# Strided and local attention ahead of an expert layer: products with v in 64x64 tiles, two pieces to a burst, with scores in bursts of their own

## The chip, the cores and the metric

One core of one Trainium2 chip runs the whole program. The metric is the device time of one execution in microseconds, the median of three runs. The matrix engine (TensorE) is PE in the rows.

## What is computed

Eight batches of 576 tokens with eight heads of 64 are attended to, four heads with a local mask (a query sees itself and the 31 keys before it) and four with a strided mask (a query sees keys at or before it in the same residue modulo 32). The result, 4608 rows of 512, goes through a two-matrix layer with a smooth gate.

```python
    mask_local = (rel >= 0) & (rel < stride)
    mask_strided = (rel >= 0) & (pos[None, :] % stride == pos[:, None] % stride)
    ...
    scores = np.where(masks[None, :, :, :], scores, -1000000000.0)
    scores = scores - np.max(scores, axis=-1, keepdims=True)
    attn = np.exp(scores)
    attn = attn / (np.sum(attn, axis=-1, keepdims=True) + 1e-09)
    return np.matmul(attn, v).astype(np.float32)
...
    h = x @ w_in
    sp = np.maximum(h, 0.0) + np.log1p(np.exp(-np.abs(h)))
    g = h * erf(sp)
    return (g @ w_out).astype(np.float32)
```

## The kernel before

**The layer.** The rows are taken in 12 chunks of 384, and the hidden width of 2048 in 16 steps of 128. A chunk and a step make an `ftile`: `mm1` (12 matmuls of 384 columns: high and low parts of x and of the weight), a chain of eight steps that ScalarE (ACT) and VectorE (DVE) do in turn, and three `mm2` jobs of three matmuls of 512 columns, which add up in one bank per 128 rows. 192 ftiles run in all. The x of a chunk lies in `xhi` and `xlo`, a ring of two batches.

**The weights** come as pairs of 32-bit words. For each of 32 weight tiles (`weight`) DVE does `bits0`, `bits1` and `bits2`, ACT the high part, and DVE the low part (`split_lo_w`, which writes `pair`).

**The attention** is cut into six pieces to a batch: local pieces of two blocks of 96 queries against 128 keys, and strided pieces of two blocks of seven residues (126 queries and keys) and a last one of four residues. A piece holds four heads, two on the partitions (`h`) and two side by side (`i`). The twelve pieces of the first two batches (`head`) run while the weights are loaded. The other 36 (`quad`) run among the ftiles of earlier batches. A quad goes: scores on PE (line 327, or line 312 for the last strided piece), `mask` (DVE), `maxi` (GpSimd, POOL), `sub` (DVE), `exp` (ACT), `total` (POOL), `gather`, `invert` and `spread` (DVE), the products with v on PE (`av`, line 574, tile `x`), `scale` (DVE), and per pair of heads a high part (ACT) and a low part (DVE) into the ring.

**The order.** `Plan.order` walks all operations with planned durations and due times (`HK`, `GK`, `WK`, ...) and writes one order for each engine; an engine never departs from it at run time. Where PE has nothing planned ahead of the first `mm1`, the plan puts in `warm` matmuls. In a quad the products of the piece before and the scores of the next are one job, so that they stand side by side:

```python
            def burst():
                yield from before.av()
                yield from g.scores()
```

**The banks.** Two banks (`ps`) take scores, three (`h`) take the results of `mm1` and the products `x`, and three take the sums of `mm2`. Scores run as 64x64 tiles of the array (64 rows of q and k for one head, 64 keys), products as 128x64 tiles (128 keys, 64 values of one head).

Of the kernel before, what the change touches and what calls it, by code (L numbers as in the profile page):

```python
# [19 lines left out]
P = 128  # L20
CH = 384
# [11 lines left out]
WK = (68.9352, -179.94, -4.88482, -99.4542, 101.236, 96.6232, -88.8363, 94.4097, 145.483, 133.702, 121.816, 123.575, 147.426, 102.135, 159.432, 198.004, -50.7856, -9.1942, 6.38548, 86.1292, 102.234, 0.760304, 78.3002, 56.9697, 173.822, 137.573, 106.312, 217.753, 188.75, 198.944, 228.222, 217.783)  # L33
LD = (5.82581, -62.2561, -111.18)
HD = (-24.4811, -111.662, -129.595, -53.3828, -157.869, -21.6826, -158.891, -9.78484, -7.41211, -95.013, -64.0153, -4.18983)
HK = (10.9721, -123.087, -70.0383, -13.5816, 91.4778, 39.4063, 92.0314, 93.8213, 94.7931, 115.323, 121.42, 178.387)
GK = (32.6682, 31.3304, 33.8245, 38.4663, 38.8279, 43.8312, 47.6315, 49.4667, 53.9059, 59.3896, 61.1923, 65.5209, 63.8285, 72.2803, 72.1316, 75.437, 80.7086, 86.9161, 80.8736, 95.711, 101.92, 105.262, 109.74, 109.871, 115.411, 120.755, 121.654, 126.517, 130.466, 137.372, 136.019, 146.264, 153.723, 151.754, 162.279, 163.399)
QD = (-3.67373, 14.2205, -4.5465, 1.44199, -4.58934)
ADT = -0.840127
PF = -5.56049  # L40
BACKLOG = 3.44486
FT = (-1.5755, -14.4223, 3.35947, -5.55073, -22.2539, 3.41975, -8.81461, 1.84242, -9.78646)
# [7 lines left out]
WE = 2 * (S - 4 * QS) + P  # L50
WV = 2 * 2 * (D + 1)
# [65 lines left out]
class Plan:  # L117
# [9 lines left out]
    WINDOW = 70  # L127
# [77 lines left out]
def attention_moe(  # L205
# [23 lines left out]
    xhi = [cpool.tile([P, RING], F32R, name=f"xhi{c}") for c in range(NCC)]  # L229
    xlo = [cpool.tile([P, RING], F32R, name=f"xlo{c}") for c in range(NCC)]  # L230
# [4 lines left out]
    cap = cpool.tile([P, 368], BF16, name="cap")[:, : 2 * QL + QS]  # L235
    cap_l = cap[:, : 2 * QL].rearrange("p (b h q) -> p b h q", b=2, h=1)
    cap_s = cap[:, 2 * QL :].rearrange("p (u q) -> p u q", u=1)
# [32 lines left out]
    def group(b, loc, j, bank="ps", spare=None):  # L270
# [20 lines left out]
        s = [buf("ps_" + bank, bank, [P, 512], f"s{i}_{pid}") for i in range(nbank)]  # L291

# [69 lines left out]
        def views(px, i, t):  # L362
            base, src = (b % 2) * S, px[:, i * w : (i + 1) * w]
            if loc:
                c0 = base + j * 2 * QL
                return src, t[:, c0 : c0 + w]
            r0 = 2 * RB * j
            dst = t[:, base : base + S].rearrange("p (a r) -> p a r", r=32)[:, :, r0 : r0 + w // NA]
            return src.rearrange("p (r a) -> p a r", a=NA), dst

        def split(px, i):
            def split_hi():
                src, hi = views(px, i, xhi[hps[i]])
                yield nc.scalar.copy(hi, src)

            def split_lo_x():
                src, hi = views(px, i, xhi[hps[i]].bitcast(F32))
                _, lo = views(px, i, xlo[hps[i]])
                yield nc.vector.tensor_tensor(out=lo, in0=src, in1=hi, op=ALU.subtract)

            return split_hi, split_lo_x
# [9 lines left out]
    def head(b, loc, j, key, dt, early, bank, num, sub_pe_too, norm_act):  # L391
# [13 lines left out]
        pt = buf("ps_h", "h", [P, 512], f"t_{pid}")  # L405
# [97 lines left out]
        done = []  # L503
        for i in range(2):
            hi, lo = g.split(pt, i)
            o = add("act", act(w, 0.07), key + 2 * dt + 0.1, hi, [o_t], [], [pt])
            done.append(add("dve", dve(w), key + 2 * dt + 0.2, lo, [o], [], [pt]))
        return done

    def quad(b, loc, j, key, dt, before):  # L510

        g = group(b, loc, j)
        n, nblk, nbank, cols, w, s, sm, pid = g.n, g.nblk, g.nbank, g.cols, g.w, g.s, g.sm, g.pid
        mx = [buf("apool", "mx", [P, 512], f"mx{i}_{pid}") for i in range(nbank)]
        su = [buf("apool", "mx", [P, 512], f"su{i}_{pid}") for i in range(nbank)]
        pos = 32 * (-(-n // 32))
        width = 32 * (-(-cols // 32)) if nbank == 2 else 2 * pos
        tt = buf("apool", "tt", [P, 512], f"tt_{pid}")
        inv = buf("apool", "tt", [P, 512], f"inv_{pid}")
        rc = buf("zpool", "r", [P, 16, 1], f"r_{pid}")  # L520
        px = buf("ps_h", "h", [P, 512], f"x_{pid}")

        def mask(k):
            def run():
                r, z, m = g.masks(k, cap_l, cap_s)
                yield nc.vector.tensor_tensor(  # L526
                    out=sm[k][:, :cols].rearrange(r, **z), in0=s[k][:, :cols].rearrange(r, **z), in1=m, op=ALU.min
                )

            return named("mask", run)  # L530

# [6 lines left out]
        def gather(h):  # L538

            def run():  # L540
                rows, t = slice(h * D, (h + 1) * D), su[h % nbank]
                tail = width - cols if nbank == 2 else pos - n
                if tail:
                    yield nc.vector.memset(t[rows, cols : cols + tail], 1.0)
                if nbank == 2:
                    yield nc.vector.transpose(tt[rows, :width], t[rows, :width])  # L546
                    return
                for u in range(2):
                    lo = (2 * u + h) * n
                    yield nc.vector.transpose(tt[rows, u * pos : (u + 1) * pos], t[rows, lo : lo + pos])  # L550

            return named("gather", run)
# [9 lines left out]
        def spread():  # L562
            nb = width // 32
            yield nc.vector.transpose(
                inv[:, :width].rearrange("p (c k) -> p c k", k=32), rc[:, :nb].broadcast_to([P, nb, 32])
            )

        def av():
            for i in range(2):
                for blk in range(nblk):  # L570
                    for h in range(2):
                        bank, c = g.place(i, blk, h)
                        c0 = (i * nblk + blk) * n
                        yield nc.tensor.matmul(  # L574
                            px[h * D : (h + 1) * D, c0 : c0 + n], g.vpart(i, blk, h, D), sm[bank][:, c : c + n],
                            start=True, stop=True,
                        )

        def scale():
            yield nc.vector.tensor_tensor(  # L580
                out=px[:, : 2 * w].rearrange("p (u q) -> p u q", q=n),
                in0=px[:, : 2 * w].rearrange("p (u q) -> p u q", q=n),
                in1=inv[:, : 2 * w].rearrange("p (u q) -> p u q", q=n) if nbank == 2
                else inv[:, :width].rearrange("p (u q) -> p u q", q=pos)[:, :, :n],
                op=ALU.mult,
            )

        add = plan.add
        lq, lv = loads(g, key)
        d_s = (0.76 if loc else 0.79) if nblk == 2 else 0.625  # L590
        d_v = (1.005 if n > QL else 0.8) if nblk == 2 else 0.39
        if before:
            def burst():
                yield from before.av()
                yield from g.scores()

            o_s = add("pe", d_s + before.d_v, key, burst, [lq, *before.need], [before.px, *s, *sm], [g.qk, *before.use])
            before.finish(o_s)
        else:
            o_s = add("pe", d_s, key, g.scores, [lq, *o_con], [*s, *sm], [g.qk])  # L600
        o_e = []
        for k in range(nbank):
            o = add("dve", dve(cols), key + 0.1 + 0.01 * k, mask(k), [o_s], [], [s[k], sm[k]])
            o = add("pool", 0.4 + cols * 0.0028, key + 0.2 + 0.01 * k, g.maxi(k, mx[k]), [o], [mx[k]], [sm[k]], earliest=6.7)
            o = add("dve", dve(cols), key + QD[0] * dt + 0.01 * k, g.sub(k, mx[k]), [o], [], [mx[k], sm[k]])
            o_e.append(add("act", act(cols), key + QD[0] * dt + 0.1 + 0.01 * k, g.exp(k), [o], [], [sm[k]]))
        o_g = []
        for k in range(nbank):
            o = add("pool", 0.094 + cols * 0.0063, key + QD[1] * dt + 0.01 * k, total(k), [o_e[k]], [su[k]], [sm[k]])
            o_g.append(o)  # L610
        n_g = (1 if nbank == 2 else 2) * 0.06 + width / 960.0 + (0.16 if cols % 32 else 0.1)
        o = None
        for h in range(2):
            k = h % nbank
            o = add("dve", n_g, key + QD[2] * dt + 0.01 * h, gather(h), [o_g[k]] + ([o] if o else []), [tt, inv] if h == 0 else [], [su[k], tt])
        o = add("dve", 0.36, key + QD[2] * dt + 0.05, invert, [o], [rc], [tt])
        o_i = add("dve", dve(width), key + QD[2] * dt + 0.06, spread, [o], [], [rc, inv])
        done = [[], []]

        def finish(o_v):  # L620
# [217 lines left out]
    def load_consts():  # L838
        yield nc.scalar.dma_start(con_f[:, :NCON], consts)
# [215 lines left out]
```

## Time and profile before

| what | value |
|---|---|
| median of three runs | 920.48 us (920.34 to 920.9) |
| span of the profiled execution | 919.3 us |
| matmuls busy (PE) | 910.6 us, 99% |
| DVE, ACT, POOL busy | 675.9, 573.0, 313.7 us |
| products with v (line 574), matmul records | 528 |
| `warm` matmuls ahead of the first `mm1` | 134 |

The span runs from the first to the last recorded instruction. What lies around it in a timed run is the difference to the median, 1.2 us. A line number is that of the kernel of the rows.

### The profile page before, as it was taken

How to read it: one execution, taken by the hardware profiler on the slowest of the kernel's cores; microseconds unless marked ns; L12 is line 12 of the kernel's file. 1: busy time of each engine (PE TensorE's matmuls, PEld its weight loads, DVE VectorE, ACT ScalarE, POOL GpSimd, SP SyncE). 2: the span in 40 equal slices, each digit the busy share in tenths (PEclk: the TensorE clock that was granted, in tenths of full speed). 3: DMA queues.
4: the chain of work that ended last, by engine and by line, in shares of the span. 5: the costliest groups of instructions: out<-in, count | busy, mean ns of one | idle time of the engine just before them, and what ended most of it. 6: DMA issues, size and time to landing. Idle time of an engine off the chain costs nothing.

```text
span 919.3 us, 16608 instructions
## 1 busy us (share of the span) xinstructions
PE 910.6 (99%) x6273; PEld 813.4 (88%) x6273; DVE 675.9 (74%) x1473; ACT 573.0 (62%) x1279; POOL 313.7 (34%) x158
## 2 busy tenths in 40 slices
PE   8999999999999999999999999999999999999998
PEld 5888999988888898889889889898989989899997
DVE  5999999678878777687767767777766767755553
ACT  4777676656566656566566556656656655655654
POOL 4341101243735346347214425373431443300000
PEclk9999999999999999999999999999999999999999
DMA  9974011221112013112102011120210210000001
GB/s 351 391 264 143 12 58 35 92 89 47 61 41 78 17 45 99 32 37 88 52 0 71 25 62 54 47 65 32 59 42 1 75 61 13 35 1 1 35 0 35
DMA packets 25712, 63.15 MB, mean 69 GB/s; under 512 B 2848, under 2 KB 4256, under 8 KB 25632
## 3 DMA queue, kind: packets, MB, share of 16 engines
q1 hardware_dynamic: 25488, 61.86, 19.8%
q8 instruction: 49, 0.80, 0.3%
q14 instruction: 31, 0.25, 0.1%
q10 hardware_dynamic: 144, 0.23, 0.1%
HBM read 51.07 MB, written 11.01 MB: 68 GB/s over the span
## 4 chain that ended last, share of the span: by engine, by line
PE 95%; DVE 3%; ACT 1%; DMA 0%; issue 0%; POOL 0%; DVEq 0%
PE o L764 42%; PE h L701 42%; PE x L574 3%; PE ps L327 2%; PE warm L936 2%; PE av L435 1%; DVE a L706 1%; PE ps L423 0%; PE ps L312 0%; PE s L423 0%; DMA qk<-qk_loc 0%; DVE sm L351 0%; PE ps L411 0%; PE t L470 0%; PE ps L435 0%; DVE w L660 0%
## 5 line engine op out<-in xcount | busy, mean ns | idle before, releaser
L709 ACT ACTIVATE a<-a 128x384 f32<-128x384 f32 x576 | 294.7, 523 | 114.5 <-DVE a L706 105.6
L764 PE MATMUL o<-pair,ghi 128*128 128x512 f32 x1154 | 359.6, 393 | 0.0
L706 DVE SCALAR_TENSOR_TENSOR a<-a,h 128x384 f32<-128x384 f32 x384 | 209.9, 549 | 140.4 <-ACT a L709 138.0
L701 PE MATMUL h<-xhi,pair 128*128 128x384 f32 x1536 | 300.1, 338 | 0.3 <-DVE glo L736 0.3
L701 PEld LDWEIGHTS h<-xhi,pair 128*128 128x128 f32 x1536 | 269.8, 188 | 10.0 <-DVE glo L736 1.7
L344 POOL PARTITION_ALL_REDUCE mx<-sm x88 | 135.3, 1560 | 414.1 <-DVE sm L526 334.2
L764 PEld LDWEIGHTS o<-pair,ghi 128*128 128x128 f32 x1154 | 212.9, 188 | 38.3
L764 PE MATMUL o<-pair,glo 128*128 128x512 f32 x577 | 224.7, 389 | 0.0
L534 POOL PARTITION_ALL_REDUCE su<-sm x66 | 178.5, 2740 | 73.5 <-ACT sm L358 48.7
L709 ACT ACTIVATE a<-h 128x384 f32<-128x384 f32 x192 | 94.2, 491 | 132.3 <-PE h L701 128.4
L701 PE MATMUL h<-xlo,pair 128*128 128x384 f32 x768 | 164.5, 336 | 0.0
L730 DVE TENSOR_TENSOR h<-a,h 128x384 f32<-128x384 f32 x192 | 106.9, 557 | 44.2 <-ACT a L709 43.6
L701 PEld LDWEIGHTS h<-xlo,pair 128*128 128x128 f32 x768 | 136.0, 188 | 0.0
L764 PEld LDWEIGHTS o<-pair,glo 128*128 128x128 f32 x577 | 108.4, 188 | 23.1
L736 DVE TENSOR_TENSOR glo<-h,ghi 128x384 fp32r<-128x384 f32 x192 | 105.9, 552 | 24.6 <-ACT ghi L733 21.2
L733 ACT CAST ghi<-h 128x384 fp32r<-128x384 f32 x192 | 90.8, 473 | 45.3 <-PE o L764 28.4
L358 ACT ACTIVATE sm<-sm 128x384 f32<-128x384 f32 (+2 forms) x77 | 42.0, 553 | 13.5 <-DVE sm L351 13.2
L351 DVE TENSOR_TENSOR sm<-sm,mx 128x384 f32<-128x384 f32 (+2 forms) x77 | 46.7, 614 | 0.1
L546 DVE STREAM_TRANSPOSE tt<-su 64x384 f32<-64x384 f32 (+1 forms) x60 | 37.4, 624 | 5.3 <-POOL su L534 2.2
L526 DVE TENSOR_TENSOR sm<-ps,cap 128x384 f32<-128x384 f32 (+2 forms) x66 | 37.4, 587 | 3.6 <-PE ps L327 2.3
L574 PEld LDWEIGHTS x<-sm,v 128*64 128x64 f32 x528 | 24.6, 136 | 9.8 <-issue 8.4
L574 PE MATMUL x<-sm,v 128*64 128x96 f32 (+2 forms) x528 | 31.7, 260 | 0.0
(62 smaller groups left out, 451.8 us busy)
## 6 DMA issues: line engine op xcount, KB each, us to landing
v<-v_all SPq DMA_DIRECT2D x40, 260.0 KB, 3.8
qk<-qk_loc SPq DMA_DIRECT2D x24, 416.0 KB, 3.4
out<-ob SPq DMA_DIRECT2D x35, 256.0 KB, 2.0
words<-w_in SPq DMA_DIRECT2D x16, 512.0 KB, 7.1
words<-w_out SPq DMA_DIRECT2D x16, 512.0 KB, 7.3
qk<-qk_str SPq DMA_DIRECT2D x16, 508.0 KB, 3.8
qk<-qk_str SPq DMA_DIRECT2D x8, 272.0 KB, 3.1
part<-ob SPq DMA_DIRECT2D x6, 256.0 KB, 2.0
```

Source lines behind the costliest of these rows:

```text
L344: yield nc.gpsimd.partition_all_reduce(mx[:, :cols], sm[k][:, :cols], P, ReduceOp.max)
L351: yield nc.vector.tensor_tensor(out=d, in0=d, in1=mx[:, :cols], op=ALU.subtract)
L358: yield nc.scalar.activation(d, src[:, :cols] if src else d, AF.Exp, scale=1.0 / D**0.5)
L534: yield nc.gpsimd.partition_all_reduce(su[k][:, :cols], sm[k][:, :cols], P, ReduceOp.add)
L574: yield nc.tensor.matmul(px[h * D : (h + 1) * D, c0 : c0 + n], g.vpart(i, blk, h, D), sm[bank][:, c : c + n], start=True, stop=True,)
L701: yield nc.tensor.matmul(ph[:, :CH], win[4 * s + cc][:, w, fs], x[cc][:, c0 : c0 + CH], start=(i == 0), stop=(i == len(terms) - 1))
L706: yield nc.vector.scalar_tensor_tensor(out=out, in0=in0, scalar=scalar, in1=in1, op0=op0, op1=op1)
L709: yield nc.scalar.activation(dst, src, func, bias=bias[i], scale=scale)
L730: yield nc.vector.tensor_tensor(out=ph[:, :CH], in0=a.tile, in1=ph[:, :CH], op=ALU.mult)
L733: yield nc.scalar.copy(ghi.tile, ph[:, :CH])
L736: yield nc.vector.tensor_tensor(out=glo.tile, in0=ph[:, :CH], in1=ghi.tile.bitcast(F32), op=ALU.subtract)
L764: yield nc.tensor.matmul(po[:, half], g[:, ts], wout[f][:, w, half], start=(f == fs0 and i == 0), stop=(f == fs1 and i == 2 and half.stop ...
```

## The change

Only quads change in what they compute with; a head merges two writes into one.

- Strided pieces have two blocks of six residues (108 queries) for the first two and two blocks of four (72 queries) for the third, so that all six pieces have two blocks and two banks. The keys of a block lie in two halves of 64 partitions, three (or two) residues in each, padded with zeros.
- Scores are 16 matmuls a piece in 64x64 tiles of 64 columns (local), 54 or 36 (strided). They are written with the key half outermost, where it was inside the block. They are a PE job of their own.
- The products of two pieces are one PE job (`products`): 16 matmuls a piece with 64 keys against 64 values, of 64, 54 or 36 columns. Each key half goes to a bank of its own, and these are the two `ps` banks. For a local piece the middle 32 queries of a block get a share from both halves: ACT copies one (`mid`), DVE adds it (`join_mid`).
- `scale` and the splits run per key half. The factors overwrite `tt`, and `inv` is gone. The ring tiles hold two pairs of heads each, so one split serves both.
- The caps come with a DMA of their own (`load_caps`). All due times are new, as is the planner's look-ahead.

```diff
+QB = 6 * NA
+HB = QB // 2
...
+        meet = ((0, 64), (32, 96)) if loc else ((0, nh), (nh, n))
...
+        def scores():
+            for part in range(2):
+                for u in range(4):
+                    i, blk = u // 2, u % 2
+                    cq, ck = i * wq + blk * n, i * wq + 2 * n + blk * (n if loc else P) + part * 64
+                    for h in range(2):
+                        rows = slice(h * D, (h + 1) * D)
+                        q0, q1 = meet[part]
+                        yield nc.tensor.matmul(
+                            s[h][part * 64 : (part + 1) * 64, u * n + q0 : u * n + q1],
+                            qk[rows, ck : ck + 64], qk[rows, cq + q0 : cq + q1],
+                            start=u == 0, stop=True, skip_group_check=True,
+                        )
...
-        if before:
-            def burst():
-                yield from before.av()
-                yield from g.scores()
-
-            o_s = add("pe", d_s + before.d_v, key, burst, [lq, *before.need], [before.px, *s, *sm], [g.qk, *before.use])
...
+        o_s = add("pe", 0.75, key, scores, [lq, *o_con, *last], [*s, *sm], [qk])
...
+    def products(pair, key, dt):
+
+        px = [buf("ps_ps", "ps", [P, 512], f"x{p}_{pair[0].b}_{pair[0].loc}_{pair[0].j}") for p in range(2)]
+
+        def av():
+            for m, g in enumerate(pair):
+                for u in range(4):
+                    for h in range(2):
+                        for p, (q0, q1) in enumerate(((0, g.na), (g.n - g.na, g.n))):
+                            rows = slice(p * 64, (p + 1) * 64)
+                            yield nc.tensor.matmul(
+                                px[p][h * D : (h + 1) * D, m * 256 + u * g.na : m * 256 + (u + 1) * g.na],
+                                g.v[rows, (2 * u + h) * (D + 1) : (2 * u + h) * (D + 1) + D],
+                                g.sm[h][rows, u * g.n + q0 : u * g.n + q1],
+                                start=True, stop=True,
+                            )
...
+        def mid(m, g):
+            def run():
+                yield nc.scalar.copy(
+                    g.tt[:, 384:512].rearrange("p (u q) -> p u q", u=4),
+                    px[1][:, m * 256 : (m + 1) * 256].rearrange("p (u q) -> p u q", u=4)[:, :, :32],
+                )
...
+        def join_mid(m, g):
+            def run():
+                x = cells(px, m, g, 0)[:, :, 32:]
+                yield nc.vector.tensor_tensor(out=x, in0=x, in1=g.tt[:, 384:512].rearrange("p (u q) -> p u q", u=4), op=ALU.add)
...
+            for p in range(2):
+                cols = 4 * (g.nb if p else g.na)
+                o = add("dve", dve(cols), key + QD[3] * dt + 0.12 + 0.01 * m, scale(m, g, p), first if p == 0 else first[:2], [], [px[p], g.tt])
+                hi, lo = split(m, g, p)
+                o = add("act", act(cols, 0.07), key + QD[4] * dt + 0.13 + 0.01 * m, hi, [o], [], [px[p]])
+                g.done[1].append(add("dve", dve(cols), key + QD[4] * dt + 0.2 + 0.01 * m, lo, [o], [], [px[p]]))
...
-WK = (68.9352, -179.94, -4.88482, -99.4542, 101.236, 96.6232, -88.8363, 94.4097, 145.483, 133.702, 121.816, 123.575, 147.426, 102.135, 159.432, 198.004, -50.7856, -9.1942, 6.38548, 86.1292, 102.234, 0.760304, 78.3002, 56.9697, 173.822, 137.573, 106.312, 217.753, 188.75, 198.944, 228.222, 217.783)
+WK = (67.5487, -148.418, 36.8869, -154.672, -255.399, 110.018, 123.581, 130.519, 16.7657, 222.711, 198.383, 120.355, 197.321, 285.192, 240.069, 207.216, -156.292, 104.167, 46.9332, -6.25954, 76.5432, 148.16, 110.823, 161.074, -20.4493, 274.699, 209.259, 238.497, 314.036, 347.411, 319.306, 420.096)
```

Where the order puts things, at the three places that matter. First PE at the start, in the kernel before: the last stretch ahead of the first `mm1` (`t` is a head's transposed result, `qk_2_0` belongs to the second batch, `warm` is a filler).

```order
L411 MATMUL ps_94<-con 128x504
...
L936 MATMUL warm<-con 128x256
...
L470 MATMUL t_2_2_771<-ident,xn_0_2_2_709 128x72
L470 MATMUL t_2_2_771<-ident,xn_0_2_2_715 128x72
...
L701 MATMUL h_804<-xhi_81,pair_744 128x384
```

The same place in the changed kernel (line 437 is a head's product with v, here of the third local piece of the first batch, and line 472 its transpose).

```order
L437 MATMUL av_0_0_2_654<-v_0_2_239,sm_0_2_468 96x65 x4
...
L413 MATMUL ps_90<-con 128x384
L791 MATMUL h_697<-xhi_81,pair_628 128x384
...
L472 MATMUL t_0_2_725<-ident,xn_0_0_2_646 128x96 x2
L472 MATMUL t_0_2_725<-ident,xn_0_0_2_655 128x96 x2
L332 MATMUL ps_89<-qk_2_0_507 64x72
```

The transposes of that piece and the scores of the second batch's first strided piece (with their mask matmuls) moved from ahead of the first `mm1` to behind it. Over the whole stretch 104 `warm` stand where 134 stood. On DVE, 66 instructions stand ahead of the low part of the first weight tile of block 0 (`pair0`, which that `mm1` reads) where 83 stood: 8 weight tiles are finished there instead of 10, four `invert` instructions fewer and half as many splits.

Second, PE among the ftiles. In the kernel before, a quad's products and the next quad's scores (`x_0_1` is the product of a local piece):

```order
L701 MATMUL h_2357<-xlo_88,pair_1887 128x384
L574 MATMUL x_0_0_2375<-sm_2_0_0_1559,v_0_0_2082 64x96
L574 MATMUL x_0_0_2375<-sm_2_0_0_1560,v_0_0_2082 64x96
...
L327 MATMUL ps_94<-qk_0_1_1155 64x64
L327 MATMUL ps_93<-qk_0_1_1155 64x64
```

In the changed kernel the scores of the two strided pieces of a pair have six rows (nine matmuls) of `mm2` between them:

```order
L542 MATMUL ps_89<-qk_False_2599 64x54
L854 MATMUL o_2_0_2595<-pair_1100,ghi_2857 128x512 x2
L854 MATMUL o_2_0_2595<-pair_1100,glo_2866 128x512
L854 MATMUL o_2_0_2603<-pair_1100,ghi_2857 128x512 x2
L854 MATMUL o_2_0_2603<-pair_1100,glo_2866 128x512
L854 MATMUL o_2_0_2617<-pair_1100,ghi_2857 128x512 x2
L854 MATMUL o_2_0_2617<-pair_1100,glo_2866 128x512
L542 MATMUL ps_90<-qk_False_2674 64x36
```

Both scores write the same two banks (`ps_89`, `ps_90`). Products and scores no longer stand side by side anywhere: 36 bursts of scores and 18 of products are each set between matmuls of the layer. Counted in an ftile's `mm1` or its three `mm2` as one step, the products stand 4 to 16 steps behind the pair's second scores, and the next scores 3 to 19 steps behind the products. Ten of the 18 pairs have only one such step between their two scores.

Third, DVE between a pair's products and the next scores, in the changed kernel (`ps_90` and `ps_89` hold the products; lines 820, 826 and 796 belong to ftiles, line 557 is the mask of the next scores).

```order
L675 TENSOR_TENSOR ps_89<-ps_89,tt_False_7754 128x216
L820 TENSOR_TENSOR h_7822<-a_7856,h_7822 128x384
L796 SCALAR_TENSOR_TENSOR a_7895<-a_7895,h_7843 128x384
L607 STREAM_TRANSPOSE tt_False_7801<-r_False_7904 128x288
L701 TENSOR_TENSOR xlo_84<-ps_90,xhi_82 128x2x18x6
L675 TENSOR_TENSOR ps_90<-ps_90,tt_False_7801 128x144
L675 TENSOR_TENSOR ps_89<-ps_89,tt_False_7801 128x144
L701 TENSOR_TENSOR xlo_84<-ps_89,xhi_82 128x2x18x6
...
L701 TENSOR_TENSOR xlo_84<-ps_89,xhi_82 128x2x18x4
...
L557 TENSOR_TENSOR sm_7_True_7966<-ps_90,cap 128x384
```

Before, the products lay in an `h` bank, and a scale and two splits (lines 580 and 379) stood here for one piece, with the mask of the next scores ahead of the splits. Now all scales and splits of two pieces stand ahead of the next scores' mask, since the banks are the same.

## Rows read from the trace of the kernel before

**Rows 1.** The page: busy time, share of the span and instructions of each engine.

```profile
PE 910.6 (99%) x6273; PEld 813.4 (88%) x6273; DVE 675.9 (74%) x1473; ACT 573.0 (62%) x1279; POOL 313.7 (34%) x158
```

**Rows 2.** The page: the chain that ended last, by engine.

```profile
PE 95%; DVE 3%; ACT 1%; DMA 0%; issue 0%; POOL 0%; DVEq 0%
```

**Rows 3.** Windows: stretch, length, busy us of five engines, granted clock, DMA share.

```profile
40.00:48.00 8.00, 8.00 (x128) 6.92 (x128) 7.86 (x25) 7.16 (x24) 1.65 (x2) 1.00 1.01 383
185.00:400.00 215.00, 215.00 (x1576) 191.50 (x1575) 163.57 (x363) 130.92 (x290) 105.70 (x51) 1.00 0.18 57
```

**Rows 4.** Timeline of PE around 450 us: start, length, line, operation, shape, count.

```profile
443.92 0.39 PE L764 MATMUL o<-pair,glo 128*128 128x512 f32 x1
444.24 1.08 PE L574 MATMUL x<-sm,v 128*64 128x126 f32 x16
445.26 0.76 PE L312 MATMUL ps<-qk 128*128 128x144 f32 x4
445.76 1.66 PE L701 MATMUL h<-xhi,pair 128*128 128x384 f32 x8
...
452.12 0.47 PE L574 MATMUL x<-sm,v 128*64 128x72 f32 x8
452.52 0.69 PE L327 MATMUL ps<-qk 64*64 64x64 f32 x32
453.15 1.66 PE L701 MATMUL h<-xhi,pair 128*128 128x384 f32 x8
```

**Rows 5.** Timeline of PE at the last products burst.

```profile
799.11 0.88 PE L574 MATMUL x<-sm,v 128*64 128x96 f32 x16
799.92 0.72 PE L764 MATMUL o<-pair,ghi 128*128 128x512 f32 x2
800.49 0.40 PE L764 MATMUL o<-pair,glo 128*128 128x512 f32 x1
800.72 0.62 PE L764 MATMUL o<-pair,ghi 128*128 128x512 f32 x2
801.18 0.39 PE L764 MATMUL o<-pair,glo 128*128 128x512 f32 x1
```

**Rows 6.** PE from 185 to 805 us by form: count, busy us, mean ns.

```profile
L574 PE MATMUL x<-sm,v 128*64 128x96 f32 x288 | 15.9, 252 | 0.0
L574 PE MATMUL x<-sm,v 128*64 128x126 f32 x192 | 13.0, 277 | 0.0
```

**Rows 7.** Timeline of PE up to the first mm1.

```profile
43.10 0.50 PE L470 MATMUL t<-ident,xn 96*128 96x96 f32 x4
43.43 0.68 PE L435 MATMUL av<-v,sm 128*72 128x65 f32 x8
44.03 0.72 PE L327 MATMUL ps<-qk 64*64 64x72 f32 x32
...
45.12 1.15 PE L936 MATMUL warm<-con 128*128 128x256 bf16 x9
46.10 0.29 PE L470 MATMUL t<-ident,xn 72*128 72x72 f32 x2
...
47.68 1.65 PE L701 MATMUL h<-xhi,pair 128*128 128x384 f32 x8
```

**Rows 8.** Timeline of DVE at the same place.

```profile
47.81 0.67 DVE L674 TENSOR_TENSOR pair<-w,pair 128x512 fp32r<-128x512 f32 x1
```

**Rows 9.** DVE from 14 to 185 us by form: count, busy us, mean ns.

```profile
L674 DVE TENSOR_TENSOR pair<-w,pair 128x512 fp32r<-128x512 f32 x32 | 23.2, 724 | 1.4 <-ACT pair L671 1.4
...
L653 DVE TENSOR_SCALAR w<-words 128x512 uint32<-128x512 uint32 x30 | 13.5, 460 | 0.1
```

**Rows 10.** Line 574: when its semaphore waits were taken up.

```profile
L574 PE MATMUL x<-sm,v x528: 226/246/323, 188.2 to 799.7; 128*64 128x96 f32 x96, 128*64 128x126 f32 x64, 128*64 128x72 f32 x16
L574 PEldq EVENT_SEMAPHORE  x36: 51/51/665, 185.3 to 795.9; - x36
```

**Rows 11.** Timeline of DVE behind the scores burst of 452.52.

```profile
453.27 1.02 DVE L526 TENSOR_TENSOR sm<-ps,cap 128x384 f32<-128x384 f32 x2
```

More of the change, by code (lines that the diff above doesn't have):

```diff
@@ L126 @@
     ENTER = 0.08
-    WINDOW = 70
+    WINDOW = 400
     def __init__(self, bufs):
@@ L502, in head @@
         o_t = add("pe", 0.22 * nblk, key + 2 * dt, transp, o_n, [pt], xn_b)
[L503 to L517, printed above, removed]
+        o = add("act", act(2 * w, 0.07), key + 2 * dt + 0.1, g.split_hi, [o_t], [], [pt])
@@ new lines, in head, with quad @@
+        return [add("dve", dve(2 * w), key + 2 * dt + 0.2, g.split_lo_x, [o], [], [pt])]
+    def quad(b, loc, j, key, dt, load, last):
+        n = QL if loc else (QB if j < 2 else 4 * NA)
+        w, cols, nh = 2 * n, 4 * n, n // 2
+        pid = f"{b}_{loc}_{j}"
+        wq = WL if loc else 2 * n + 2 * P
+        wv = 4 * (D + 1)
+        width = 32 * (-(-cols // 32))
+        na, nb = (64, 32) if loc else (nh, nh)
+        qk = buf("apool", "qk", [P, 2 * WS], f"qk_{pid}")
+        v = buf("zpool", "v", [P, 2 * WV], f"v_{pid}")
+        s = [buf("ps_ps", "ps", [P, 512], f"s{i}_{pid}") for i in range(2)]
+        sm = [buf("apool", "sm", [P, 512], f"sm{i}_{pid}") for i in range(2)]
+        mx = [buf("apool", "mx", [P, 512], f"mx{i}_{pid}") for i in range(2)]
+        su = [buf("apool", "mx", [P, 512], f"su{i}_{pid}") for i in range(2)]
@@ L523, in mask @@
         def mask(k):
             def run():
[L525 to L528, printed above, removed]
-            return named("mask", run)
+                d, x = sm[k][:, :cols], s[k][:, :cols]
+                if loc:
+                    m = (cap_l if j == 0 else cap_l[:, 1:2]).rearrange("p b h q -> p h b q").broadcast_to([P, 2, 2, n])
+                    d, x = (y.rearrange("p (i b q) -> p i b q", i=2, b=2) for y in (d, x))
+                else:
+                    m = cap_s.rearrange("p (u t q) -> p u t q", u=1, t=2)[:, :, :, :nh].broadcast_to([P, 4, 2, nh])
+                    d, x = (y.rearrange("p (u t q) -> p u t q", u=4, t=2) for y in (d, x))
@@ L532, in total, with exp, run @@
+        def exp(k):
+            def run():
+                d = sm[k][:, :cols]
+                yield nc.scalar.activation(d, d, AF.Exp, scale=1.0 / D**0.5)
+            return named("exp", run)
         def total(k):
@@ L540, in run @@
             def run():
[L541 to L550, printed above, removed]
+                rows, t = slice(h * D, (h + 1) * D), su[h]
+                if width > cols:
+                    yield nc.vector.memset(t[rows, cols:width], 1.0)
+                yield nc.vector.transpose(tt[rows, :width], t[rows, :width])
             return named("gather", run)
@@ L564, in spread @@
             yield nc.vector.transpose(
[L565 to L585, printed above, removed]
+                tt[:, :width].rearrange("p (c k) -> p c k", k=32), rc[:, :nb].broadcast_to([P, nb, 32])
@@ L601, in quad @@
-        o_e = []
[L602 to L606, printed above, removed]
+        lq = add("sp", P * 8 * wq / 3.6e5, load - LD[0], load_qk, new=[qk])
@@ new lines, in quad @@
+        lv = add("sp", P * 8 * wv / 3.6e5, load - LD[1], load_v, new=[v])
+        o_s = add("pe", 0.75, key, scores, [lq, *o_con, *last], [*s, *sm], [qk])
+        o_e = []
+        for k in range(2):
+            o = add("dve", dve(cols), key + 0.1 + 0.01 * k, mask(k), [o_s, *o_cap], [], [s[k], sm[k]])
+            o = add("pool", 0.4 + cols * 0.0028, key + 0.2 + 0.01 * k, maxi(k), [o], [mx[k]], [sm[k]])
+            o = add("dve", dve(cols), key + QD[0] * dt + 0.01 * k, sub(k), [o], [], [mx[k], sm[k]])
+            o_e.append(add("act", act(cols), key + QD[0] * dt + 0.1 + 0.01 * k, exp(k), [o], [], [sm[k]]))
@@ L607, in quad @@
         o_g = []
[L608 to L611, printed above, removed]
+        for k in range(2):
+            o_g.append(add("pool", 0.094 + cols * 0.0063, key + QD[1] * dt + 0.01 * k, total(k), [o_e[k]], [su[k]], [sm[k]]))
+        n_g = 0.06 + width / 960.0 + (0.16 if cols % 32 else 0.1)
@@ L618, in quad @@
-        done = [[], []]
-        def finish(o_v):
-            done[0].append(o_v)
-            o_x = add("dve", dve(2 * w), key + QD[3] * dt + 0.1, scale, [o_v, o_i], [], [px, inv])
-            for i in range(2):
-                hi, lo = g.split(px, i)
-                o = add("act", act(w, 0.07), key + QD[4] * dt + 0.1, hi, [o_x], [], [px])
-                done[1].append(add("dve", dve(w), key + QD[4] * dt + 0.2, lo, [o], [], [px]))
+        o_i = add("dve", dve(width), key + QD[2] * dt + 0.06, spread, [o], [], [rc, tt])
@@ L918, in attention_moe @@
             else:
-                a = quad(b, loc, j, PRO + SLOT * GK[6 * b + i - 12], ADT * SLOT, quads[-1][0] if quads else None)
+                k = 6 * b + i - 12
+                a = quad(
+                    b, loc, j, PRO + SLOT * GK[k], ADT * SLOT, PRO + SLOT * AK[k // 2] + k % 2, [quads[-1][0].o_s] if quads else []
+                )
                 quads.append((a, b // 2, to))
-    a = quads[-1][0]
-    a.finish(plan.add("pe", a.d_v, a.key, a.av, a.need, [a.px], a.use))
+                if k % 2:
+                    products((quads[-2][0], quads[-1][0]), PRO + SLOT * AK[k // 2], ADT * SLOT)
     for a, p2, to in quads:
@@ L989, in _layout @@
     vs = vs.reshape(B, 2, 2, S, D)
+    qk_new, v_new = np.zeros_like(qk_str), np.zeros_like(v_all[:, 1])
+    for j in range(3):
+        n = QB if j < 2 else 4 * NA
+        nh, wq = n // 2, 2 * n + 2 * P
+        qb = np.zeros((B, P, 2, wq), f32)
+        vb = np.zeros((B, P, 2, 2, 2, D + 1), f32)
+        for blk in range(2):
+            for p in range(2):
+                p0 = (12 * j) * NA + (2 * p + blk) * nh
+                for i in range(2):
+                    qb[:, :, i, blk * n + p * nh : blk * n + (p + 1) * nh] = qs[:, i, :, p0 : p0 + nh]
+                    k0 = 2 * n + blk * P + p * 64
+                    qb[:, :, i, k0 : k0 + nh] = ks[:, i, :, p0 : p0 + nh]
+                    for h in range(2):
+                        vb[:, p * 64 : p * 64 + nh, i, blk, h, :D] = vs[:, i, h, p0 : p0 + nh]
+        qk_new[:, j, :, : 2 * wq] = qb.reshape(B, P, 2 * wq)
+        v_new[:, j, :, : 8 * (D + 1)] = vb.reshape(B, P, 8 * (D + 1))
     for j in range(3):
```

146 lines of the change are left out of this document (102 added, 44 removed).

## The prediction

> **What bounds the kernel now.** I first read the engines' busy shares: PE is busy for 99% of the span, DVE for 74% [rows 1]. The chain that ended last agrees: 95% of it is PE work [rows 2]. Then I looked at stretches: from 185 to 400 us PE is busy in every microsecond, at the full clock (1.00, the 2.4 GHz level), while DVE has a quarter of its time free; from 40 to 48 us DVE is busy for 7.86 of 8 us [rows 3]. So among the ftiles time is won only by PE work that goes away, and lost only by a new PE wait. At the start the fillers hide how long PE really waits, and DVE, which prepares the weights, is nearly full.
>
> **What a burst costs before.** In the timeline of PE [rows 4] the last mm2 starts at 443.92. Matmuls of its kind start 0.23 apart (800.49 to 800.72 [rows 5]), so the burst could begin at 444.15 and begins at 444.24: 0.09 to enter. Two mm2 matmuls behind a burst take 0.57 where the next two take 0.46 [rows 5]: 0.11 to leave. A border pair thus costs 0.20. Between them the products take 1.02 with 126 columns (444.24 to 445.26), 0.40 with 72 (452.12 to 452.52), 0.81 with 96 (799.11 to 799.92); scores take 0.63 in 64x64 tiles (452.52 to 453.15) and 0.50 as four wide matmuls (445.26 to 445.76) [rows 4, 5].
>
> A piece of 96 or 126 columns has 16 records and one of 72 has 8, so 288 and 192 records are 18 and 12 pieces, and the 48 that are left of 528 are 6 [rows 6, 10]. Products: 18 x 0.81 + 12 x 1.02 + 6 x 0.40 = 29.2. Scores: 30 x 0.63 (I count the strided ones like the local ones) + 6 x 0.50 = 21.9. Borders: 36 x 0.20 = 7.2. Sum 58.3 us.
>
> **What it costs after.** Two 128x64 tiles work side by side, so 16 records are 8 steps. From 96 to 126 columns the burst grows by 0.21, 0.9 ns for each step and column; the 72-column burst of 4 steps then gives a step of 0.082 at 96 columns and 0.16 that is paid once per burst. A scores burst of 32 records in four tiles is 8 steps: (0.63 - 0.16) / 8 = 0.059 each. The new products have two times 8 such steps: 0.16 + 16 x 0.059 = 1.10 a pair. For 54 and 36 columns no row exists. The 0.9 ns would take 0.009 and 0.025 off a step (192 steps of the one, 96 of the other: 4.0 us in all); a floor on the step would take nothing off. I take nothing, the value of the nearest row (64 columns), and keep the 4.0 for the low end.
>
> A sentence of the Trainium skill bears on this: TensorEngine Tiling (Array Packing), section Performance Considerations, says that a matmul has some 60 cycles of overhead, so that fewer columns than that save nothing; by it the sum stays, by the slope of the rows it is 4.0 lower. No row shown here has fewer than 64 columns, so none decides it.
>
> After: scores 36 x 0.63 = 22.7, products 18 x 1.10 = 19.8, borders 54 x 0.20 = 10.8 (18 bursts more, since products and scores stand apart). Sum 53.3. **Term 1: -5.0 us.**
>
> **The start.** 30 fillers fewer stand ahead of the first mm1. Nine take 0.98 (45.12 to 46.10), 0.109 each: 3.3 us [rows 7]. The third local piece's transposes (0.33, 43.10 to 43.43) and one head's scores with masks (1.09, 44.03 to 45.12) are only moved behind it. If data comes in time, the first mm1 starts at 47.68 - 3.3 - 1.4 = 43.0. Does DVE allow it? Its low part of the first weight runs at 47.81, with the first mm1 [rows 8]: it is as late as PE is. Ahead of it two weight tiles go, four instructions each of 0.46 to 0.72 [rows 9], 5.1 us at their middle, and about 1 us of inverts and splits. That covers the 4.7 us. But the two tiles are done later, at a DVE that stays full; the second mm2 job reads one of them. I take 1.0 us of waiting for it, between none and the whole 3.3. **Term 2: -3.3 + 1.0.** The caps' DMA stands sixth on SP's queue, ahead of a load of v; DVE's wait for it falls where it waits for early loads anyway. I cost it at nothing; its cover is that wait, and without cover it is one transfer smaller than the others.
>
> **The new waits.** Both scores of a pair and its products use the same two banks. (a) The second scores need both masks of the first. Before, two masks began 0.12 behind the burst and took 1.02 (453.27, burst end 453.15) [rows 11], so the banks are free 1.1 to 1.2 behind the scores, and up to 0.7 later where DVE is inside another instruction [rows 9]. The shortest step between is nine mm2, 9 x 0.23 = 2.1. Ten pairs have that little. Behind a waiting score matmul stands all PE work, ftiles too. (b) The next scores need the last split. DVE's scales and splits of two pieces and the ftile instructions among them (the third order excerpt) are some 13 instructions of 0.3 to 0.6, about 5; at least three ftile steps, 6 us, stand between. (c) Products need the second scores' mask, maximum, subtraction and exponential, and at least four steps, 8 us, stand between. I take 1.0 us in all for (a) to (c), between 0 and 7 (0.4 for each of 18 pairs). **Term 3: +1.0.**
>
> **The rest** is hidden: join_mid, mid and one more scale and its fixed part per piece are some 8 us of DVE and 3 of ACT over 600 us in which DVE is idle for a quarter [rows 3]; without that cover they would cost just these 8. Loads change by about one part in fifty. The ftiles get three `h` banks to themselves, worth nothing while PE does not wait.
>
> **Sum.** 919.3 - 5.0 - 3.3 + 1.0 + 1.0 = 913.0. The median of the runs lies 1.2 above the span, so **914.2 us**.
>
> **Rivals.**
> - *Key half outermost halves the overlap of tiles* (the other side). The first 16 records of a scores burst now use only the two tiles of one key half, the last 16 the other two. If PE does not start a matmul past earlier ones that wait for their tiles, 8 steps become 16: 8 x 0.059 = 0.47 a burst, 17 us over 36, and the time is 931. From 0.17 a burst (three steps) on the change loses. Against it: the queue takes the wait of a products burst up at 185.3, 2.9 us ahead of its first matmul at 188.2 [rows 10], some 13 to 16 matmuls, so the other half's matmuls are queued when the burst starts. Whether one may pass another no row says outright. The Trainium skill speaks for the rival: TensorE: Matmul & The Clock Gate, section Part 3: Packing small matmuls — row/col tiling, has matmuls start and end strictly in program order; read so, this burst is 16 steps. Yet the bursts before, with four tiles, are 8 steps. 13%.
> - *The banks give it back.* Waits (a) and (b) come to 0.4 a pair, 7 us in place of 1: 920. For it: three users on two banks; against it the spaces of 2, 6 and 8 us. A start that yields nothing (917) goes with it. 19%.
> - *Narrow tiles are faster* by the slope: 910.2. 12%.
> - The forecast, 911 to 917: 56%.
>
> **How the numbers follow.** Range 909.0 to 920.5: the narrow case and nearly all of the giving back are inside, the first rival is not. 0.2% (1.8 us) is about what a measurement here can tell. Faster: the forecast, the narrow case and half of the giving back, 0.77; within 0.2% the other half, 0.10; slower the first rival, 0.13.
>
> **What would show it.** Right: products bursts of 1.1 us from start to next mm, scores bursts of 0.6; the first mm1 near 43; PE waits on DVE or ACT at scores under 2 us in all. Wrong: scores of 1.1 (first rival); PE waits at scores or products of 0.3 and more per pair; a wait on DVE's `glo` or `pair` behind the first mm1 of 3 us. It fails too if products of two pieces take over 1.3, since then separate borders eat the gain.

## The result, and the profile after

The changed kernel takes 929.41 us (median of 4 runs, 928.95 to 929.74) beside 920.67 (920.34 to 920.9) for the kernel before: the ratio is 1.0093, 95% interval 1.0079 to 1.0108. It is slower by 8.7 us, where 914.2 was predicted and 909.0 to 920.5 allowed. One run among all that follow, a run of e6 that took 4,928 us, is left out. The span of the profiled execution is 927.2, so 7.9 us more than before and 14.2 more than the prediction's 913.0.

The page of the kernel after, busy time and the chain that ended last:

```profile
PE 914.3 (99%) x7035; PEld 813.1 (88%) x7035; DVE 678.4 (73%) x1503; ACT 574.0 (62%) x1291; POOL 316.4 (34%) x170
...
PE 93%; ACT 2%; DVE 2%; DMA 1%; POOL 1%; issue 0%; ACTq 0%; POOLq 0%
```

PE is busy 3.7 us longer than in [rows 1], and of the 7.9 us the other 4.2 is PE's idle time (12.9 in place of 8.7). On the chain PE has lost two points and DVE one; ACT, DMA and POOL have gained one each [rows 2]. So there are two things to find: bursts that are longer than was thought, and new waits.

Timeline of PE after: scores bursts of 36, 64 and 54 columns, each with the row behind it, and one products burst with the rows around it:

```profile
243.13 0.93 PE L542 MATMUL ps<-qk_False 64*64 64x36 f32 x32
243.98 0.50 PE L854 MATMUL o<-pair,ghi 128*128 128x512 f32 x1
...
262.01 0.86 PE L791 MATMUL h<-xlo,pair 128*128 128x384 f32 x4
262.80 1.14 PE L644 MATMUL ps<-sm_False,v_False 64*64 64x54 f32 x64
263.87 0.74 PE L854 MATMUL o<-pair,ghi 128*128 128x512 f32 x2
...
272.34 0.97 PE L542 MATMUL ps<-qk_True 64*64 64x64 f32 x32
273.25 0.74 PE L854 MATMUL o<-pair,ghi 128*128 128x512 f32 x2
...
285.18 0.96 PE L542 MATMUL ps<-qk_False 64*64 64x54 f32 x32
286.07 0.45 PE L791 MATMUL h<-xhi,pair 128*128 128x384 f32 x1
```

Read from start to start. The local scores burst takes 0.91 us (272.34 to 273.25), where the same 32 records in the same tiles took 0.63 in [rows 4]; the strided ones take 0.89 and 0.85. The products burst takes 1.07 for two strided pieces, near the 1.10 that was predicted. PE's waits after (two of 0.3 and 0.2 us, also at heads, are left out):

```profile
PE ps L332 <- DMA qk<-qk_loc: 5.1, 1, 5.1
PE ps L437 <- ACT sm L363: 1.4, 2, 1.0
PE o L854 <- ACT ob L896: 1.4, 1, 1.4
PE h L791 <- DVE glo L826: 0.4, 1, 0.4
...
```

The first row is the start of the program (4.3 before). None of the others is at a quad's scores or products, where the prediction's third term and second rival put them. They are at a head's products, at a bank of `mm2` and at an `mm1`. The first of them is in the timeline of PE after, behind the first `mm1`:

```profile
44.50 1.70 PE L791 MATMUL h<-xhi,pair 128*128 128x384 f32 x8
...
46.73 0.49 PE L472 MATMUL t<-ident,xn 96*128 96x96 f32 x4
...
48.06 1.75 PE L791 MATMUL h<-xhi,pair 128*128 128x384 f32 x8
49.65 0.86 PE L791 MATMUL h<-xlo,pair 128*128 128x384 f32 x4
51.49 0.38 PE L437 MATMUL ps<-v,sm 128*96 128x65 f32 x2 [0.99 <-ACT sm L363]
52.32 1.40 PE L437 MATMUL ps<-v,sm 128*96 128x65 f32 x14 [0.44 <-ACT sm L363]
53.53 0.95 PE L791 MATMUL h<-xhi,pair 128*128 128x384 f32 x4
```

The first `mm1` starts at 44.50, against 47.68 in [rows 7]. PE stands 1.43 us at 51 us, for the exponentials of a head piece. The second wait is at 122 us. Here is PE there, then ACT, then SP's queue, each a timeline of the kernel after:

```profile
122.19 0.39 PE L854 MATMUL o<-pair,glo 128*128 128x512 f32 x1
123.99 0.73 PE L854 MATMUL o<-pair,ghi 128*128 128x512 f32 x2 [1.41 <-ACT ob L896]
```

```profile
123.36 0.58 ACT L896 COPY ob<-o 128x512 f32<-128x512 f32 x1 [2.89 <-DMA part<-ob]
```

```profile
117.23 0.33 SPq L737 DMA_DIRECT2D words<-w_out  x1
117.66 0.39 SPq L905 DMA_DIRECT2D part<-ob  x1
```

ACT stands 2.89 us because the `ob` buffer that it must write is still being stored: the store issued at 117.66 stands 0.43 behind a load of 512 KB of weights, and the copy starts 5.7 us after that issue. ACT's work of the ftiles stands behind it, and PE waits for the bank that ACT would empty. In the kernel before the same load also went ahead of the second store, but by 3.2 us, and nothing waited (timeline of SP's queue before):

```profile
116.21 0.33 SPq L647 DMA_DIRECT2D words<-w_out  x1
119.41 2.57 SPq L815 DMA_DIRECT2D part<-ob  x2
```

### The profile page after: what moved, and what is told of

Its sections match the earlier page's. It is cut to its first block, busy times and chain, and to the rows that moved or that the text cites. A ratio compares the mean times of both kernels' runs of the same rounds, so it can differ in the third digit from the quotient of the medians.

```text
span 927.2 us, 18128 instructions
## 1 busy us (share of the span) xinstructions
PE 914.3 (99%) x7035; PEld 813.1 (88%) x7035; DVE 678.4 (73%) x1503; ACT 574.0 (62%) x1291; POOL 316.4 (34%) x170
## 4 chain that ended last, share of the span: by engine, by line
PE 93%; ACT 2%; DVE 2%; DMA 1%; POOL 1%; issue 0%; ACTq 0%; POOLq 0%
PE h L791 42%; PE o L854 41%; PE ps L542 3%; PE ps L644 2%; ACT a L799 1%; PE warm L1034 1%; PE ps L437 1%; DMA part<-ob 1%; POOL su_True L583 0%; DMA qk<-qk_loc 0%; DMA words<-w_in 0%; PE av L437 0%; PE ps L332 0%; PE s L425 0%; DVE a L796 0%
## 5 line engine op out<-in xcount | busy, mean ns | idle before, releaser
L563 POOL PARTITION_ALL_REDUCE mx_True<-sm_True x36 | 51.3, 1455 | 227.0 <-DVE sm_True L557 171.2
L826 DVE TENSOR_TENSOR glo<-h,ghi 128x384 fp32r<-128x384 f32 x192 | 105.3, 549 | 16.5 <-ACT ghi L823 14.2
L583 POOL PARTITION_ALL_REDUCE su_True<-sm_True x36 | 90.6, 2556 | 44.1 <-DVE sm_True L570 24.6
L563 POOL PARTITION_ALL_REDUCE mx_False<-sm_False x36 | 51.1, 1448 | 151.4 <-DVE sm_False L557 133.7
L583 POOL PARTITION_ALL_REDUCE su_False<-sm_False x36 | 90.9, 2567 | 19.1 <-ACT sm_False L577 14.4
L349 POOL PARTITION_ALL_REDUCE mx<-sm x22 | 34.1, 1563 | 51.5 <-ACT sm L419 16.6
L696 ACT CAST xhi<-ps 128x128 fp32r<-128x128 f32 (+3 forms) x72 | 21.3, 323 | 11.3 <-DVE ps L675 9.8
L593 DVE STREAM_TRANSPOSE tt_False<-su_False 64x448 f32<-64x448 f32 (+1 forms) x36 | 20.9, 579 | 6.4 <-POOL su_False L583 4.3
L896 ACT COPY ob<-o 128x512 f32<-128x512 f32 x35 | 20.2, 583 | 8.2 <-PE o L854 3.4
```

Source lines behind the costliest of these rows:

```text
L349: yield nc.gpsimd.partition_all_reduce(mx[:, :cols], sm[k][:, :cols], P, ReduceOp.max)
L563: yield nc.gpsimd.partition_all_reduce(mx[k][:, :cols], sm[k][:, :cols], P, ReduceOp.max)
L583: yield nc.gpsimd.partition_all_reduce(su[k][:, :cols], sm[k][:, :cols], P, ReduceOp.add)
L826: yield nc.vector.tensor_tensor(out=glo.tile, in0=ph[:, :CH], in1=ghi.tile.bitcast(F32), op=ALU.subtract)
```

## The experiments

Two theories of the longer scores bursts were set against each other. A matmul of these bursts shows as two records (16 matmuls, 32 records); one record is called a pass here. Theory A: a tile takes only a few passes ahead of the one that runs, and behind them the whole sequence stands, so that with the key half outermost the second half's tiles begin late. Theory B: the bursts are longer for another reason (shape, banks, neighbours). All kernels but `e4` are the changed one with the edit shown.

**e1: the key half inside the block again.**

```diff
-            for part in range(2):
-                for u in range(4):
+            for u in range(4):
+                for part in range(2):
```

> The changed kernel with one thing undone: the 16 matmuls of a scores burst are written with the block outermost and the key half inside it, as before the change. Everything else, the order of jobs too, stays. Theory A (a tile of the array takes only about three matmul passes ahead of the one that runs; behind them the sequence stands, so the second key half's tiles stay idle until the first half has three passes left): with the half inside, all four tiles run from the start, scores bursts fall from 0.91 to 0.63 us, 36 x 0.26 = 9.4 us, and the time is 920.0. Rival B (the longer scores bursts come from the change of shape, banks or neighbours, not from the order inside the burst): scores stay at 0.9, time 929.4.

Measured: 918.93 us, ratio to before 0.9974 (0.9964 to 0.9985). Timeline of PE, a local burst and strided ones of 54 and 36 columns, each with the row behind it:

```profile
270.64 0.69 PE L542 MATMUL ps<-qk_True 64*64 64x64 f32 x32
271.27 0.73 PE L854 MATMUL o<-pair,ghi 128*128 128x512 f32 x2
...
238.80 0.69 PE L542 MATMUL ps<-qk_False 64*64 64x54 f32 x32
239.41 0.73 PE L854 MATMUL o<-pair,ghi 128*128 128x512 f32 x2
241.68 0.67 PE L542 MATMUL ps<-qk_False 64*64 64x36 f32 x32
242.28 0.73 PE L854 MATMUL o<-pair,ghi 128*128 128x512 f32 x2
```

The local burst takes 0.63. How the tiles fill is seen in the first 0.21 us of a strided burst (windows of line 542 alone: stretch, length, PE and PEld busy with records, clock, DMA share, GB/s). First the kernel after, in a second row its first 0.29 us, then e1:

```profile
285.18:285.39 0.21, 0.21 (x6) 0.21 (x8) 1.00 0.98 371
285.18:285.47 0.29, 0.29 (x10) 0.29 (x12) 1.00 0.99 374
```

```profile
283.16:283.37 0.21, 0.21 (x12) 0.21 (x16) 1.00 1.03 390
```

Six passes have started after, twelve in e1: two tiles work where four could. After 0.29 us it is ten, five for each of two tiles; the next passes to start, 0.01 later, are the second half's first ones, while three of the eight passes of each first tile still wait. Theory A stands, B falls. The 54 and 36 columns give 0.61 and 0.60: fewer columns save next to nothing.

**e2, e5: runs of two and of three blocks.** The halves alternate after two blocks (four passes to a tile), or after three and then one. The edit shown is that of e2.

```diff
-            for part in range(2):
-                for u in range(4):
+            for part, us in ((0, (0, 1)), (1, (0, 1)), (0, (2, 3)), (1, (2, 3))):
+                for u in us:
```

> The changed kernel with the key half alternating after every two blocks: each tile gets runs of four passes (two matmuls) in place of eight. Theory A (three passes may be pending on a tile): a run of four is one that runs and three that wait, so nothing stands behind it; bursts of 0.63 us and 920.0, as with the block outermost. Rival C (each run of one half costs in proportion to its length): half of the loss stays, bursts of 0.76, 924.7. Rival B: 929.4.

> The changed kernel with three blocks of one key half in a row, then three of the other, then the last block of each: runs of six passes to a tile. Theory A: the second half starts when the third pass of the first half starts, 0.098 + 0.058 = 0.16 late, and nothing is lost behind that; bursts of 0.63 + 0.15 = 0.78, 36 x 0.15 = 5.4 above the order with the block outermost (918.9): 924.3. Rival C (loss in proportion to the run, 0.28 for eight passes and 0.04 for four as measured): about the same, 0.16; so this run checks the size. A rule by which only the number of matmuls between two of the same half counts, with all or none lost, would give 0.62 or 0.89.

Measured: 920.33 us for two blocks (0.9992, 0.9983 to 1.0001) and 925.03 for three (1.0046, 1.0033 to 1.006). A local burst in the timeline of PE of each, two blocks first:

```profile
270.83 0.74 PE L542 MATMUL ps<-qk_True 64*64 64x64 f32 x32
271.51 0.74 PE L854 MATMUL o<-pair,ghi 128*128 128x512 f32 x2
```

```profile
272.38 0.86 PE L542 MATMUL ps<-qk_True 64*64 64x64 f32 x32
273.17 0.73 PE L854 MATMUL o<-pair,ghi 128*128 128x512 f32 x2
```

0.68 and 0.79 us. The run of three blocks loses 0.16, as theory A had it. The run of two loses 0.05 where A said nothing, a step or less; why is open.

**e6: one tile after the other.**

```diff
-            for part in range(2):
-                for u in range(4):
+            for part, h in ((0, 0), (0, 1), (1, 0), (1, 1)):
+                for u in range(4):
...
-                    for h in range(2):
```

> The changed kernel with the four tiles of a scores burst written one after the other: eight passes for one tile, then eight for the next. Theory A1 (three passes may wait on each tile, whatever waits on others): each next tile starts when the fifth pass of the one ahead starts, 0.27 later; burst 0.62 + 3 x 0.27 = 1.44, time 918.9 + 36 x 0.82 = 948.4. Theory A2 (six passes may wait in all, for two tiles that is three each): the second tile starts with the third pass of the first, 0.16 late, the third tile at 0.36 and the fourth at 0.55; burst 1.18, time 939. Strictly one after the other would give 1.9 us.

Measured: 948.25 us (1.0299, 1.0284 to 1.0315). The local burst:

```profile
274.81 1.54 PE L541 MATMUL ps<-qk_True 64*64 64x64 f32 x32
276.28 0.73 PE L853 MATMUL o<-pair,ghi 128*128 128x512 f32 x2
```

1.47 us, 0.84 above e1: three times 0.28. So three passes wait on each tile by itself (A1), not six in all.

**e3: the products' key half outermost too.**

```diff
-            for m, g in enumerate(pair):
-                for u in range(4):
-                    for h in range(2):
-                        for p, (q0, q1) in enumerate(((0, g.na), (g.n - g.na, g.n))):
+            for p in range(2):
+                for m, g in enumerate(pair):
+                    for u in range(4):
+                        for h in range(2):
+                            q0, q1 = ((0, g.na), (g.n - g.na, g.n))[p]
```

> The changed kernel with its scores as they are, and the products of a pair also written with the key half outermost, over both pieces: each tile gets a run of 16 passes. Theory A: the second half's tiles start when the thirteenth pass of the first half starts, 0.098 + 11 x 0.058 = 0.74 us late; products bursts of 1.08 + 0.74 = 1.82 us, 18 x 0.74 = 13.3 us more, 942.7. Strictly serial halves would give 2.0 us and 946. Rival B (the loss belongs to scores alone): 1.08 and 929.4.

Measured: 940.11 us (1.0207, 1.0193 to 1.0221), 10.7 above the changed kernel. A products burst of two strided pieces:

```profile
263.64 1.86 PE L645 MATMUL ps<-sm_False,v_False 64*64 64x54 f32 x64
265.43 0.73 PE L855 MATMUL o<-pair,ghi 128*128 128x512 f32 x2
```

1.79 us in place of 1.07: 0.72 more, as theory A has it. The total grew by less than 18 x 0.74 = 13.3. The row of PE waiting for `glo`, 0.4, is not among this kernel's waits, and its first PE work is 0.36 earlier; the rest of the difference is open.

**e4: the kernel before, with its scores' key half outermost.**

```diff
...
+            steps = [(i, blk, part) for i in range(2) for blk in range(2) for part in range(2)]
+            if b >= 2:
+                steps.sort(key=lambda x: x[2])
+            for i, blk, part in steps:
...
```

> The kernel before, with the key half outermost in the scores of its 30 quads of two blocks (64, 62 and 72 columns), nothing else. Theory A: 18 local bursts lose 0.26 and 12 strided ones five steps of 0.058 to 0.063, so 0.28: 8.0 us, 928.5. Rival B: 920.5.

Measured: 928.85 us (1.0085, 1.0069 to 1.01), as theory A has it. A local burst:

```profile
264.31 0.98 PE L330 MATMUL ps<-qk 64*64 64x64 f32 x32
265.22 0.73 PE L767 MATMUL o<-pair,ghi 128*128 128x512 f32 x2
```

0.91, the very figure of the kernel after: two swapped loops alone make the kernel before as slow as the changed one.

**e7: e1 with a store ahead of a load** on SP's queue at 116 us. The numbers are places in the plan's order; the load moves behind the store.

```diff
+    seq = plan.order()
+    seq.insert(673, seq.pop(671))
...
```

> The changed kernel with the block outermost, and on SP's queue the load of the last weight tile moved behind the store of the second kept sum of 128 rows. Theory D: ACT's copy of the third kept sum waited from 120.4 to 123.3 for that store to land, behind 512 KB of weights, and PE 1.7 us for the copy; with the store ahead the wait is gone and the time is 918.9 - 1.6 = 917.3. Rival: the wait moves to the weight, which lands later and is needed by the last step of the block; 918.9.

Measured: 917.48 us (0.9965, 0.9953 to 0.9977). The interval overlaps that of e1, so the gain over e1 (1.4 us between the medians, 0.8 by the ratios) is not settled by the times; the trace is plainer. PE waits for `ob` no more, and ACT copies without a pause:

```profile
119.62 0.57 ACT L896 COPY ob<-o 128x512 f32<-128x512 f32 x1
```

With e8, which the times do not tell from it, it is the fastest of the kernels here, some 0.35% below the one before.

**e8: e7 with a head piece's softmax ahead of weight work**, at the wait of 51 us.

```diff
-    seq.insert(673, seq.pop(671))
+    for src, dst in ((671, 673), (335, 332), (330, 328), (330, 327), (321, 302), (312, 302)):
+        seq.insert(dst, seq.pop(src))
```

> The kernel with the store ahead, and also: POOL's two maxima of the first piece of batch 1 are written ahead of three weight instructions of DVE (POOL is made to wait for the last such instruction written ahead of it), the second subtraction ahead of a weight's low part, and the two exponentials ahead of two steps of an ftile. Theory E: PE's wait of 1.4 us at that piece's products (51 us) comes from POOL's maximum, which starts 1.3 us behind its data; 0.9 of the wait goes, 916.4, and the trace shows the products' waits at 0.5. Rival: what the weights and ftiles lose there comes back as a wait elsewhere in the next 10 us; 917.3.

Measured: 917.36 us (0.9967, 0.9954 to 0.9979), no gain over e7. Three timelines of e8, of POOL, DVE and PE:

```profile
46.20 3.29 POOL L349 PARTITION_ALL_REDUCE mx<-sm  x2 [5.72 <-DVE w L756]
```

```profile
46.41 1.20 DVE L750 SCALAR_TENSOR_TENSOR w<-words,w 128x512 uint32<-128x512 uint32 x1
...
50.12 1.01 DVE L356 TENSOR_TENSOR sm<-sm,mx 128x384 f32<-128x384 f32 x2
```

```profile
51.58 0.38 PE L437 MATMUL ps<-v,sm 128*96 128x65 f32 x2 [1.07 <-ACT sm L363]
52.37 1.40 PE L437 MATMUL ps<-v,sm 128*96 128x65 f32 x14 [0.41 <-ACT sm L363]
```

POOL starts 1.7 us behind the first `mm1` (44.52 in this run); in e7 it is 3.3. But DVE's instruction beside it takes 1.20 us, and the subtractions, whose maxima end at 49.49, stand in DVE's own queue until 50.12. PE's wait is 1.48, as long as before. The same instruction and the first maximum in e7, DVE and then POOL:

```profile
45.66 0.69 DVE L750 SCALAR_TENSOR_TENSOR w<-words,w 128x512 uint32<-128x512 uint32 x1
```

```profile
47.05 1.42 POOL L349 PARTITION_ALL_REDUCE mx<-sm  x1 [7.32 <-DVE pair L764]
```

So with the maximum earlier, DVE's work is 0.5 longer, on an engine that has no time to spare here. Theory E, that the wait comes from POOL's maximum, falls: what POOL gains is lost in DVE's queue.

The delay itself was there all along. In e1, as in the kernel after and in e7, it falls on the first subtraction (DVE, then POOL):

```profile
49.26 1.02 DVE L356 TENSOR_TENSOR sm<-sm,mx 128x384 f32<-128x384 f32 x1
```

```profile
49.05 1.42 POOL L349 PARTITION_ALL_REDUCE mx<-sm  x1 [0.18 <-DVE w L756]
```

The subtraction starts 0.21 behind a maximum of POOL and takes 1.02, where two of e8 take 1.01 together. e8 has moved the delay from the subtraction to `bits1` of a weight. Both times a DVE instruction ran beside POOL's maximum; no run here tests why that makes it longer.

## Why the prediction was wrong

**The step that failed is in Term 1: "After: scores 36 x 0.63 = 22.7".** The price was of the nearest row, but with another order of the same 16 matmuls; what that order costs was left to a rival and stood in the sum at nothing. After, the burst takes 0.91 at 64 columns and 0.89 and 0.85 at 54 and 36: some 0.26 too much for each of 36, 9.4 us, more than the whole gain. e1 takes 0.25 to 0.28 a burst away by the order alone, and e4 puts 0.28 on the local bursts of the kernel before.

**The first rival had the mechanism and the wrong price, and its time came near by luck.** It said that the first half's tiles work alone. What it missed is that the second half starts when three passes of the first are still pending: the loss is 0.25 to 0.28 a burst and not 0.47. With that loss alone, some 9.8 us, it would have said 924 and not 931; the measured 929 is made up by the start and the waits, of which it said nothing. The argument that was raised against it, that the queue takes up work 13 to 16 matmuls ahead [rows 10], speaks of the queue ahead of the array. What counts is what may wait on one tile, which is three passes. Its point of breaking even, 0.17 a burst, came from a gain of 6.3 us that was not there. The run of two blocks, which loses 0.05, is already level with the kernel before, and the run of three (0.16) is 4.5 us slower.

The Trainium skill's page TensorE: Matmul & The Clock Gate, section Part 3: Packing small matmuls — row/col tiling, on which that rival leaned, has matmuls start strictly in program order. The rows do not bear that out across tiles: in such an order the burst would take 16 steps (1.1 us), and it takes 0.91, because the second half's matmuls start ahead of passes of the first that still wait. As a warning against this loop order the rule pointed the right way.

**The rest of Term 1 held.** Products of two pieces take 1.07 where 1.10 was said. Narrow tiles save next to nothing (0.61 and 0.60 beside 0.63), so the third rival falls. The Trainium skill's page TensorEngine Tiling (Array Packing), section Performance Considerations, by which fewer than some 60 columns save nothing, agrees with the rows. Entering is as cheap as before: four `mm1` matmuls from 262.01 at the spacing of 0.174 end at 262.70, and the burst starts at 262.80. Eighteen more borders at 0.20 remain what the split costs.

**Term 2 was too good by about 2.6 us.** The first `mm1` came 3.2 earlier and not 4.7; 0.8 of what is missing lies at the very start, where the first scores waited 5.1 for their load and not 4.3. Behind it the head's work cost 3.5 us more: 1.3 moved (46.73 to 48.06), 1.4 of waiting at 51 us, and 0.5 that the job, broken in two by the waits, takes beyond them (from 50.34, where four `mm1` matmuls from 49.65 end, to 53.53 is 3.2, and the same job takes 1.3 where it does not wait); the rest is small. So the start gave nothing. The prediction had DVE as late as PE and put 1.0 us on a weight. DVE was late indeed, but the wait came at a piece's softmax, whose subtractions stand in DVE's queue between weights, and it was longer. The one other order that was tried (e8) does not buy it back. Writing the weight work later was not tried.

**Term 3 was right about the banks and missed two other waits.** The scores and products of quads wait nowhere for the two banks, so 0 in place of 1.0. But the new order brought a store to 0.43 behind a weight's load, where 3.2 lay between (1.6 us: 122.19 to 123.99 in place of 0.23; e7 takes the wait away), and a pair's split ahead of an ftile's `glo` on DVE (0.4; the kernel before has waits for `glo` of 0.3 and 0.4 elsewhere).

The sum for the span: bursts +4.0 (36 x 0.89 + 18 x 1.08 + 54 x 0.20 = 62.3, beside 58.3), start +0.3, waits among the ftiles +3.0 (the store 1.6, `glo` 0.5, the rest in pieces of 0.1 to 0.3), together 7.3 of the 7.9; 0.6 is not placed. Against the predicted span the miss is 14.2: scores 9.4, start 2.6, waits 2.0 (3.0 in place of 1.0), the 0.6, less 0.4 for the products. With the loops swapped back and the store ahead, e7 stands 3.3 above the predicted 914.2; 2.6 of it is the start by the trace of the kernel after, and some 2 by its own, whose first `mm1` starts at 43.77. The rest of the change is thus worth its place, if only by 0.26% (e1); the loop order turned it into a loss.

## What to carry to other kernels

When small matmuls run in several tiles of the array, deal them out in turn: in this burst two in a row on one tile cost 0.05 us, three 0.16, four 0.28, and one nothing; the instructions' count alone does not give a burst's time. A price taken from a row holds only for the same order inside the burst. A new order of jobs needs a look at every queue: here a store that came close behind a load cost as much as eight borders.

## What was not expected of the hardware

A tile of the array lets three passes wait behind the one that runs, each tile by itself; the fourth holds up the whole sequence. This one number gives the loss at runs of 6, 8 and 16 passes. By single records a tile's second pass starts 0.098 behind its first at 54 columns (0.107 at 64), and each later one 0.058 behind the one before; from the 54 columns 0.16, 0.27 and 0.74 are worked out, and 0.16, 0.28 and 0.72 are measured. For four tiles in a row it is 0.84, against 3 x 0.27. It does not give the 0.05 at runs of four, and what in the array holds the passes up is not shown. All of this was seen with 64x64 tiles and single-precision data of 36 to 64 columns.
